# Gated mix of two attentions: projections in four column tiles, other buffer counts, and a last set in halves

## The chip, the cores and the metric

The kernel runs on one core of one Trainium2 chip. The metric is device time in microseconds (us) of one execution; lower is better. All times below come from runs on the chip or from one profiled execution.

## The reference

For x of 2048 rows and 512 columns (bf16) the reference computes `g * a + (1 - g) * b`:

```python
g = sigmoid((x * gate_w).sum(-1, keepdims=True))
# a, linear attention, 32 heads of 16:
pq, pk = q @ w_phi, k @ w_phi                      # per head, 16 x 16
phi_q = concat([softmax(pq), softmax(-pq)], -1)    # phi_k alike from pk
kv, z = einsum("bhsf,bhsd->bhfd", phi_k, v), phi_k.sum over s
a = (phi_q @ kv) / (phi_q @ z + 1e-6)  -> (2048, 512) @ A_wo
# b, softmax attention, 32 heads of 16:
b = softmax(q @ k.T * 0.25) @ v        -> (2048, 512) @ B_wo
```

Part b holds nearly all the work: 32 x 2048 x 2048 scores, an exponential of each, and the product with v.

## The kernel before, in words

**The softmax attention.** It runs in 32 sets (loop at L802 to L806): four blocks `qc` of 512 queries, four groups `g` of eight heads, and for each two halves `par` of four heads. A set has 16 key tiles `kt` of 128 keys; a key tile of a set is two score tiles of 128 keys x 1024 (two heads x 512 queries), so there are 32 x 16 x 2 = 1024 score tiles.

- Scores (`qk`, L826): two matmuls in row tiles (64 rows each) fill a PSUM tile of ring `R_r`, which has three of 1024 columns (L427). The zeros in the query tile `q` separate the heads.
- Exponentials, on one of two engines. ScalarE (ACT) does most with one ACTIVATE per score tile (L849) into a ring `E_r` of NE = 8 buffers of 128 x 1024 (L402); the first 24 go to memory of phiK and vA that isn't used yet. For `NDVE[set]` key tiles of each set VectorE (DVE) does them with integer steps: L839 for each of the two score tiles, then L861, L864 and L867 on 2048 columns. NDVE sums to 123 key tiles, so DVE does 246 score tiles and ACT 778.
- Weighted sums (`pv`, L873 and L886): four matmuls in column tiles (32 columns of weights each, `tile_position=(0, 32 * s)`) add to the one PSUM bank `O_r`, one group for a key tile on ACT, two for one on DVE.
- End of a set: O is copied out (L512 or L513, called at L911), transposed by TensorE (four f32 transposes, L918), and DVE takes the reciprocal of the row sums (L923) and multiplies (L924). The result goes by a DMA transpose (L939) to `oBT`; for the last set of all it goes by four transposes on TensorE (L949) and two copies (L952).

**Beside it.** Projections for q, k, v, the feature maps and A's v: `fill` (L515) issues four accumulating matmuls with 128 x 128 weights and 512 columns of x each (L519), and is called for 81 tiles (324 matmuls). The 16 output blocks take seven matmuls each (`of`, L974) and an eighth (`os`, L982) when the last head group is there; the result is scaled (L987 on ACT, L990 on DVE) and written (L992). The feature maps take two ACT exponentials for each of 32 blocks (L700), adds on GpSimd (POOL, L706) and more. A query tile is made by a projection, a copy to `qs`, and eight small DMAs on the SyncE queue (SP, L567) into a ring of four `q` buffers (L400), of which three are zeroed by POOL (L490).

**What sets the order.** Nothing is ordered by hand. `_Sched` (L108) is a list scheduler that runs before the program is built: each operation has an engine, an estimated duration, a due time (`prio`, mostly a time `ut(u)` in the plan of the 32 sets), dependencies, and, where it is first to use a ring buffer, a wait for the last user of that buffer. For TensorE the pick also weighs how many score tiles ACT and DVE have ahead, how many E buffers are held (`FULL`, L149), and a price `STAY` for a change of mode between "row", "col" and "full". The result is one fixed order of instructions per engine, with semaphore waits. So every constant at L35 to L81 can move every operation, and the time on the chip comes from the fixed orders alone.

**The check at the end.** L997 to L1002 test all the sums (DVE, DVE, TensorE, DVE) and write a flag; each engine waits for it, and a slow safe version of the kernel would follow if it were set. Here it isn't.

Of the kernel before, what the change touches and what calls it, by code (L numbers as in the profile page):

```python
# [6 lines left out]
BF16 = mybir.dt.bfloat16  # L7
# [3 lines left out]
ALU = mybir.AluOpType  # L11
# [5 lines left out]
KT = 4  # L17
S = 2048
NT = S // 128
NQ = 512  # L20
QC = S // NQ
# [14 lines left out]
PH = [0.0, -2.7, 0.0, 0.0, -1.2, 0.0, 1.2, 0.0, -0.7, -1.4, -1.5, -2.2, -2.9, -3.8, 2.5, -1.5, -1.5, -2.3, 0.7, -3.8, -0.7, -4.5, -2.0, -0.8, 0.0, -6.0, 5.8, 0.0, 0.1, 6.1, 3.6, 1.4]  # L36
# [5 lines left out]
NE = 8  # L42
FULL = 7
FEW = 1
SLACK = 0.6
# [6 lines left out]
RUSH_K = 20.0  # L52
RUSH_O = 10
RUSH_1 = 8.0
QLEAD1 = 26
LATE_A = 10
VLEAD = 3.0
VLEAD1 = 24
RUSH_V = 20.0
PK0 = 170  # L60
PKS = 20
PQ0 = 470
PQS = 30
KLEAD1 = 28
KLEAD = 40
QLEAD = 36
EARLY = 4
# [13 lines left out]
LATER = 14.0  # L81
# [26 lines left out]
class _Sched:  # L108
# [9 lines left out]
    def add(self, eng, prio, dur, fn, deps=(), tiles=(), mode=None, name="", dma=None, nb=0.0, after=(), parts=1, feeds=None):  # L118
        o = _Op()
        o.eng, o.fn, o.dur, o.prio = eng, fn, dur, prio  # L120
        o.deps = [d for d in deps if d is not None]
        o.after = list(after)
        o.tiles = list(tiles)
        o.mode, o.name, o.dma, o.est = mode, name, dma, nb
        o.shared = eng == "pool" or name in ("dm", "de", "dw") or name.startswith("qm")
        o.frees = any(t.slots is self.stock for t in tiles)
        o.late = 0.0 if name.startswith("qk") else SLACK
# [230 lines left out]
def _build(ctx, nc, A_x, A_wqkv, A_w_phi, A_wo, B_wqkv, B_wo, gate_w, out):  # L358
# [30 lines left out]
    ident = sb([128, 128], name="ident")  # L389
# [10 lines left out]
    q_r = ring(4, [128, 4, NQ], name="q")  # L400
# [63 lines left out]
    def pool(prio, dur, fn, deps=(), name="", nb=0.0):  # L464
        return add("pool", prio, dur, fn, deps=deps, name=name, nb=nb)
# [15 lines left out]
    op_id32 = i2  # L481
# [8 lines left out]
    op_qz = [pool(-96 - 0.1 * i, 2.0, lambda e, i=i: e.memset(q_r.aps[i][:], 0.0), name="qz", nb=LATER + 3.0) for i in range(1, 4)]  # L490
# [7 lines left out]
    MM = 0.217  # L498
# [15 lines left out]

    def fill(prio, tile, off, lhs, rhs, deps, name, rush=0.0, xd=None, n=512):  # L515

        f = None
        for t in range(KT):
            f = add("pe", prio - rush + 0.01 * t, MM * n / 512, lambda e, t=t: e.matmul(  # L519
                tile.ap[:, off:off + n], lhsT=lhs(t), rhs=rhs(t), start=(t == 0), stop=(t == KT - 1)),  # L520
                deps=list(deps) + (xd(t) if xd else []) + [f], tiles=[tile], mode="full", name=name, nb=max(0.0, prio - EARLY))
            fills.append(f)
        return f
# [210 lines left out]
    op_kz = []  # L734
# [67 lines left out]
    for qc in range(QC):  # L802
        for g in range(KT):
            ob = _Tile(oB_r)
            norm = []
            for par in range(2):  # L806
# [104 lines left out]
                n1 = evac("act" if final else "dve", ut(u) - RUSH_O, lambda ot=ot: ot.ap, lambda O=O: O.ap,  # L911
                          pvs + [op_m4, op_masks], [O, ot], name="Oev")

                if nset == 31:
                    calm = norm
                n2 = []
                for i in range(4):
                    n2.append(add("pe", pr, 0.165, lambda e, i=i, ot=ot, tt=tt: e.transpose(  # L918
                        tt.ap[:, 128 * i:128 * (i + 1)], ot.ap[:, 128 * i:128 * (i + 1)], ident32[:]),
                        deps=[n1, op_id32], tiles=[ot, tt], mode="full", name="tpb"))  # L920
                tv = lambda tt=tt: tt.ap[:, 0:512].rearrange("p (i s c) -> p i s c", i=4, c=32)
                rv = lambda rb=rb, part=part: rb.ap[:, part, :].rearrange("p (a b) -> p a b", b=4)
                n3 = add("dve", pr, 0.17, lambda e, tv=tv, rv=rv: e.reciprocal(rv(), tv()[:, :, :, 16]), deps=n2, tiles=[tt, rb])  # L923
                norm.append(add("dve", pr, 0.34, lambda e, tv=tv, rv=rv, ob=ob, par=par: e.tensor_tensor(  # L924
                    ob.ap.rearrange("p i (s a d) -> p i s a d", a=2, d=16)[:, :, :, par, :], tv()[:, :, :, 0:16],
                    rv().unsqueeze(3).to_broadcast([128, 4, 4, 16]), ALU.mult), deps=[n3], tiles=[tt, rb, ob]))
                recs.append(n3)
                reads.append(norm[-1])
# [8 lines left out]
            pr = ut(u + 4)  # L937
# [5 lines left out]
            to = _Tile(R_r)  # L943

            def tpc(e, ob=ob, to=to):
                ins = None
                for i in range(4):
                    v = to.ap[:, 512 * (i // 2) + 64 * (i % 2):][:, 0:64].bitcast(BF16)
                    ins = e.transpose(v, ob.ap[:, i, :], ident[:])  # L949
                return ins  # L950
            n6 = add("pe", pr, 0.45, tpc, deps=norm + [op_id], tiles=[ob, to], mode="full", name="tpc")
            ev_oBT[qc, g] = [add(eng, pr, 0.3, lambda e, to=to, g=g, qc=qc, lo=lo, eng=eng: (e.copy if eng == "act" else e.tensor_copy)(  # L952
                oBT[qc].ap[:, g, lo:lo + 256], to.ap[:, 2 * lo:2 * lo + 128].bitcast(BF16)),
                deps=[n6] + (op_kz if qc >= 2 else []), tiles=[to, oBT[qc]], name="oBev") for eng, lo in (("dve", 0), ("act", 256))]
# [6 lines left out]
    ends = [_Tile(R_r)] * 2 + [_Tile(M_r), _Tile(R_r)]  # L961
    begin = [ut(U - 6), ut(U - 6), ut(U - 4), ut(U) + 4]
    for st in range(NT):
# [8 lines left out]
        for k in range(2 * KT - 1):  # L972
            lhs, rhs = (oAT[:, k, sl], WoA[:, k, :]) if k < KT else (None, WoB[:, k - KT, :])
            f1 = add("pe", prio + 0.01 * k, MM, lambda e, tile=tile, off=off, k=k, qc=qc, sb_=sb_, lhs=lhs, rhs=rhs: e.matmul(  # L974
                tile.ap[:, off:off + 512], lhsT=lhs if k < KT else oBT[qc].ap[:, k - KT, sb_], rhs=rhs, start=(k == 0), stop=False),
                deps=[f1, ev_oAT[st], op_woA, op_woB] + [ev_oBT[qc, g] for g in range(KT - 1)], tiles=[tile, oBT[qc]],
                mode="full", name="of", nb=prio - EARLY,
                     after=[] if not last else calm if i == 2 else last_di if i < 2 else last_qk)

        def second(e, tile=tile, off=off, st=st):  # L980
            sb_ = slice(128 * (st % 4), 128 * (st % 4 + 1))
            return e.matmul(tile.ap[:, off:off + 512], lhsT=oBT[st // 4].ap[:, KT - 1, sb_], rhs=WoB[:, KT - 1, :], start=False, stop=True)  # L982
        f2 = add("pe", ut(U + 2) if last else prio, MM, second, deps=[f1, ev_oBT[qc, KT - 1][i // 2] if last else ev_oBT[qc, KT - 1]], tiles=[tile, oBT[qc]], mode="full", name="os")
        fi = _Tile(fin_r)
        src = lambda tile=tile, off=off: tile.ap[:, off:off + 512]
        if last and i % 2:
            ev = add("act", ut(U + 3), 0.478, lambda e, fi=fi, src=src, st=st: e.activation(  # L987
                fi.ap, src(), ACTF.Copy, scale=omg[:, st:st + 1]), deps=[f2, op_omg] + use_wp1, tiles=[tile, fi], name="fin")
        else:
            ev = add("dve", ut(U + 3) if last else prio, 0.66, lambda e, fi=fi, src=src, st=st: e.tensor_scalar(  # L990
                fi.ap, src(), omg[:, st:st + 1], None, op0=ALU.mult), deps=[f2, op_omg] + use_wp1, tiles=[tile, fi], name="fin")
# [5 lines left out]
    v1 = add("dve", ut(U + 2), 0.2, lambda e: e.tensor_single_scalar(acc[:, 0:144], acc[:, 0:144], BIG, ALU.is_le), deps=chk[-1:] + chkB[-1:] + [op_ge] + use_ez)  # L997
# [185 lines left out]
```

## Time and profile before

| | us |
|---|---|
| median of 3 runs | 772.44 |
| lowest and highest | 771.83 and 772.62 |
| the profiled execution, its time | 771.53 |
| the profiled execution, its span | 769.7 |
| busy: ACT, PE, DVE, POOL | 753.2, 707.5, 705.8, 182.8 |

The span runs from the first to the last event on the core; the time of the execution is 1.83 us longer. PE is TensorE's matmul row and PEld its weight loads. Records of ACT and PE overlap: an instruction's record starts before the one ahead has ended, so the mean of a record is longer than the distance from one to the next, and busy time is the union. The granted TensorE clock was 0.998.

### The profile page before, as it was taken

What the parts mean: (1) busy time and instruction counts of PE and PEld (TensorE: products, weight loads), DVE (VectorE), ACT (ScalarE), POOL (GpSimd) and SP (SyncE); (2) the same over time, 40 slices, a digit from 0 to 9 for tenths busy, and PEclk for the clock granted to TensorE, in tenths of its full rate; (3) what the DMA queues carried; (4) which work ended last, traced back from release to release, by engine and by line L of the source; (5) the groups of instructions that cost most, each with busy time, mean ns of one, the idle gap of its engine ahead of it and who ended that gap; (6) DMA issues with size and microseconds to landing.
All of it is one profiled execution on the core that took longest, in us unless ns stands there. A gap on an engine that the chain in (4) does not pass through costs nothing.

```text
span 769.7 us, 14300 instructions
## 1 busy us (share of the span) xinstructions
PE 707.5 (92%) x5880; PEld 236.7 (31%) x5949; DVE 705.8 (92%) x891; ACT 753.2 (98%) x856; POOL 182.8 (24%) x283
## 2 busy tenths in 40 slices
PE   8999999999998999999999899999999999998887
PEld 4333333332222322222233233232232323332222
DVE  6898997799999899999999989999997999999993
ACT  5999999999999999999999999999999999999995
POOL 2500000003334433343431231203311151202200
PEclk9999999999999999999999999999999999999999
DMA  9300000000000000000013112100211012100200
GB/s 220 55 9 2 15 2 1 15 2 8 8 7 9 2 15 1 15 1 8 9 15 90 21 35 36 24 26 8 48 35 29 23 28 55 28 19 18 43 8 30
DMA packets 54918, 19.60 MB, mean 25 GB/s; under 512 B 46784, under 2 KB 54848, under 8 KB 54848
## 3 DMA queue, kind: packets, MB, share of 16 engines
q1 hardware_dynamic: 53264, 18.10, 11.3%
q8 instruction: 47, 0.77, 0.4%
q10 hardware_dynamic: 1328, 0.52, 0.3%
q14 instruction: 23, 0.19, 0.1%
q0 software_dynamic: 256, 0.02, 0.1%
HBM read 4.21 MB, written 2.10 MB: 8 GB/s over the span
## 4 chain that ended last, share of the span: by engine, by line
ACT 84%; PE 11%; DMA 1%; DVE 1%; issue 1%; SPq 1%
ACT E L849 78%; PE ps L830 4%; ACT WAT L700 4%; PE ps L974 2%; PE ps L890 2%; ACT phiK L849 1%; ACT vA L849 1%; DMA D<-in_A_x_dram 1%; PE ps L877 1%; PE ps L519 1%; PE ps L742 1%; SPq L567 1%; DVE D L839 0%; DMA q<-qs 0%; PE ps L581 0%
## 5 line engine op out<-in xcount | busy, mean ns | idle before, releaser
L849 ACT ACTIVATE E<-ps 128x1024 bf16<-128x1024 f32 x754 | 702.0, 1183 | 0.4 <-PE ps L830 0.2
L830 PE MATMUL ps<-q,kT 64*128 64x512 bf16 x2048 | 361.5, 384 | 42.2 <-ACT E L849 30.3
L839 DVE TENSOR_SCALAR D<-ps 128x1024 int16<-128x1024 f32 x246 | 298.7, 1214 | 34.2 <-PE ps L830 30.7
L830 PEld LDWEIGHTS ps<-q,kT 64*128 64x128 bf16 x2048 | 90.1, 93 | 250.0 <-ACT E L849 191.7
L864 DVE TENSOR_TENSOR D<-D 128x2048 bf16<-128x2048 bf16 x123 | 151.3, 1232 | 0.6
L890 PE MATMUL ps<-E,vB 128*32 128x512 bf16 x1508 | 145.3, 388 | 3.7 <-issue 1.8
L706 POOL TENSOR_TENSOR WAT<-WAT 128x512 f32<-128x512 bf16 (+2 forms) x96 | 73.1, 762 | 260.8 <-DVE D L864 92.4
L877 PE MATMUL ps<-D,vB 128*32 128x512 bf16 x984 | 95.0, 387 | 3.4 <-issue 2.0
L861 DVE TENSOR_SCALAR D<-D 128x2048 int16<-128x2048 int16 x123 | 85.1, 694 | 0.7
L867 DVE TENSOR_SCALAR D<-D 128x2048 int16<-128x2048 int16 x123 | 83.5, 681 | 0.3
L890 PEld LDWEIGHTS ps<-E,vB 128*32 128x32 bf16 x1508 | 36.9, 93 | 76.1 <-issue 68.2
L717 POOL TENSOR_TENSOR phiK<-WAT,ss 128x512 bf16<-128x512 bf16 x32 | 33.5, 1057 | 37.5 <-DVE D L864 16.5
L519 PE MATMUL ps<-Wp,xT 128*128 128x512 bf16 x106 | 41.1, 389 | 0.5 <-issue 0.3
L700 ACT ACTIVATE WAT<-ps 128x512 bf16<-128x512 f32 x64 | 40.2, 771 | 0.0
L717 POOL TENSOR_TENSOR WB<-WAT,ss 128x512 bf16<-128x512 bf16 x32 | 33.3, 1057 | 28.0 <-DVE D L864 15.8
L519 PE MATMUL ps<-xT,WB 128*128 128x512 bf16 (+2 forms) x109 | 38.6, 380 | 0.6 <-issue 0.3
L877 PEld LDWEIGHTS ps<-D,vB 128*32 128x32 bf16 x984 | 24.4, 94 | 41.2 <-issue 35.0
L931 POOL TENSOR_TENSOR acc<-acc,rB 128x64 f32<-128x64 f32 x8 | 2.6, 320 | 120.2 <-DVE D L861 53.0
L974 PE MATMUL ps<-phiK 128*128 128x512 bf16 x80 | 28.3, 387 | 1.7 <-ACT WAT L700 1.2
L918 PE MATMUL ps<-ident,OT 128*128 128x128 f32 x128 | 27.8, 300 | 2.3 <-ACT WAT L700 1.8
L513 DVE COPY OT<-ps 128x512 f32<-128x512 f32 x31 | 21.0, 679 | 1.8 <-PE ps L890 1.6
L519 PEld LDWEIGHTS ps<-Wp,xT 128*128 128x128 bf16 x128 | 12.0, 96 | 31.8 <-issue 27.7
(100 smaller groups left out, 363.1 us busy)
## 6 DMA issues: line engine op xcount, KB each, us to landing
out_dram<-Wp SPq DMA_DIRECT2D x16, 128.0 KB, 1.7
q<-qs SPq DMA_DIRECT2D x120, 16.0 KB, 1.8
WB<-in_B_wqkv_dram SPq DMA_DIRECT2D x3, 384.0 KB, 5.4
D<-in_A_x_dram SPq DMA_DIRECT2D x1, 512.0 KB, 6.9
WAv<-in_A_wqkv_dram SPq DMA_DIRECT2D x1, 512.0 KB, 5.2
phiK<-in_A_wo_dram SPq DMA_DIRECT2D x1, 512.0 KB, 4.1
phiK<-in_B_wo_dram SPq DMA_DIRECT2D x1, 512.0 KB, 5.0
D<-in_A_x_dram ACTq DMA_DIRECT2D x1, 256.0 KB, 3.8
```

Source lines behind the costliest of these rows:

```text
L519: f = add("pe", prio - rush + 0.01 * t, MM * n / 512, lambda e, t=t: e.matmul(tile.ap[:, off:off + n], lhsT=lhs(t), rhs=rhs(t), start=(t = ...
L700: o5 = [add("act", prio + 1, 0.478, lambda e, a=a: e.activation(ev()[:, :, a, :], P(), ACTF.Exp, scale=1.0 - 2.0 * a), deps=[f], tiles=[ti ...
L706: o6 = add("pool", prio + 5, d, lambda e, n=n: e.tensor_tensor(tr(n), tr(2 * n)[:, :, 0:n], tr(2 * n)[:, :, n:2 * n], ALU.add), deps=[o6] ...
L717: halves.append(add("pool", prio + 7 + 0.1 * h, 0.15 + 1.8 / PH2, lambda e, gs_=gs_: e.tensor_tensor(dst().rearrange("p (g f) -> p g f", f ...
L830: ins = e.matmul(r.ap[:, 512 * i:512 * (i + 1)], lhsT=kT[p0:p0 + 64, g, 128 * kt:128 * (kt + 1)], rhs=qt.ap[p0:p0 + 64, 2 * pair + par, :] ...
L839: last_di = [add("dve", when - 6, 1.133, lambda e, r=r, I=I, part=part: e.tensor_scalar(I.ap[:, 1024 * part:1024 * (part + 1)], r.ap, EXP_ ...
L849: exps.append(add("act", when, 0.904, lambda e, r=r, E=E: e.activation(E.ap, r.ap, ACTF.Exp, scale=EXP_SCALE), deps=[q], tiles=[r, E], nam ...
L861: d1 = [add("dve", pd + 0.01 * y, 0.06 + 0.54 / SM, lambda e, I=I, F=F, lo=lo, hi=hi: e.tensor_scalar(F.ap[:, lo:hi], I.ap[:, lo:hi], 0x00 ...
L864: d4 = [add("dve", pd + 0.05 + 0.01 * y, 0.06 + 1.07 / SW, lambda e, I=I, F=F, lo=lo, hi=hi: e.tensor_tensor(F.ap[:, lo:hi].bitcast(BF16), ...
L867: d2 = [add("dve", pd + 0.1 + 0.01 * y, 0.06 + 0.54 / SE, lambda e, I=I, lo=lo, hi=hi: e.tensor_scalar(I.ap[:, lo:hi], I.ap[:, lo:hi], -12 ...
L877: ins = e.matmul(O.ap[32 * s:32 * s + 32, :], lhsT=vB_[:, kt, vcol(h):vcol(h) + 32], rhs=w.ap.bitcast(BF16)[:, base + 1024 * (s % 2) + 512 ...
L890: ins = e.matmul(O.ap[32 * s:32 * s + 32, :], lhsT=vB_[:, kt, vcol(h):vcol(h) + 32], rhs=es[s % 2].ap[:, 512 * (s // 2):512 * (s // 2 + 1) ...
```

## The change

1. `fill`, `of` and `os` issue each matmul as four, one for each 32 columns of the weights, with `tile_position` as `pv` has it. The planner counts them as mode "col" and takes 0.226 for 0.217.
2. NE from 8 to 12 (FULL from 7 to 11) and the ring of q from 4 to 2 buffers, so POOL zeroes one and not three.
3. The last set is finished in two halves: two copies of O of 256 columns on ACT, then for each half two transposes, reciprocal, multiply, two bf16 transposes and one copy (first half ACT, second DVE). The two halves of the last transpose go to different PSUM tiles (`t15`, which the fourth output block uses too, and O's bank).
4. Of the last four output blocks, the third is ordered behind the end of set 31 only (before: of 31 and 32, since `calm` was the list itself), and the fourth may start at `ut(U)`. The priorities of the last set's operations are earlier, and the check's first operation is planned behind the last copies.
5. NDVE, PH (offsets of DVE's key tiles in each set) and some twenty constants of the planner are changed. NDVE now sums to 124.

```diff
-NDVE = [3, 4, 3, 5, 2, 3, 4, 4, 4, 4, 4, 3, 5, 4, 3, 5, 3, 4, 4, 4, 4, 5, 4, 2, 5, 4, 3, 5, 4, 3, 5, 4]
+NDVE = [3, 5, 3, 5, 2, 4, 4, 4, 4, 4, 4, 2, 5, 4, 4, 5, 4, 4, 4, 3, 4, 5, 3, 3, 5, 5, 3, 3, 4, 3, 5, 4]
...
-NE = 8
-FULL = 7
+NE = 12
+NQB = 2
+FULL = 11
...
-STAY = 1.8
-RUSH = 2.5
+STAY = 1.0
+RUSH = 2.0
...
-    q_r = ring(4, [128, 4, NQ], name="q")
+    q_r = ring(NQB, [128, 4, NQ], name="q")
...
+    def by_columns(e, out_ap, lhs, rhs, start, stop):
+        ins = None
+        for s in range(4):
+            ins = e.matmul(out_ap[32 * s:32 * s + 32, :], lhsT=lhs[:, 32 * s:32 * s + 32], rhs=rhs, start=start, stop=stop,
+                           tile_position=(0, 32 * s), skip_group_check=True)
+        return ins
...
-                    pvs.append(add("pe", at, 0.226, term, deps=deps + op_vpad, tiles=tiles, mode="col", name=f"pv{nset}"))
-                pr = ut(u + 2)
+                    pvs.append(add("pe", at - (15.0 if nset == 32 else 0.0), 0.226, term, deps=deps + op_vpad, tiles=tiles, mode="col", name=f"pv{nset}"))
+                pr = ut(u - 16) if final else ut(u + 2)
...
+                nh = 2 if final else 1
+                w = 4 // nh
+                for hh in range(nh):
+                    lo = 128 * w * hh
...
                 if nset == 31:
-                    calm = norm
+                    calm = list(norm)
...
-    ends = [_Tile(R_r)] * 2 + [_Tile(M_r), _Tile(R_r)]
-    begin = [ut(U - 6), ut(U - 6), ut(U - 4), ut(U) + 4]
+    ends = [_Tile(R_r)] * 2 + [_Tile(M_r), t15]
+    begin = [ut(U - 6), ut(U - 6), ut(U - 4), ut(U)]
```

More of the change, by code (lines that the diff above doesn't have):

```diff
@@ L126, in add @@
         o.frees = any(t.slots is self.stock for t in tiles)
-        o.late = 0.0 if name.startswith("qk") else SLACK
+        o.late = 0.0 if name.startswith("qk") or name in ("tpc", "end") else SLACK
         o.users, o.start, o.end, o.count, o.sem, o.vc = [], None, None, None, None, None
@@ L518, in fill @@
         for t in range(KT):
-            f = add("pe", prio - rush + 0.01 * t, MM * n / 512, lambda e, t=t: e.matmul(
-                tile.ap[:, off:off + n], lhsT=lhs(t), rhs=rhs(t), start=(t == 0), stop=(t == KT - 1)),
-                deps=list(deps) + (xd(t) if xd else []) + [f], tiles=[tile], mode="full", name=name, nb=max(0.0, prio - EARLY))
+            f = add("pe", prio - rush + 0.01 * t, MM * n / 512, lambda e, t=t: by_columns(
+                e, tile.ap[:, off:off + n], lhs(t), rhs(t), t == 0, t == KT - 1),
+                deps=list(deps) + (xd(t) if xd else []) + [f], tiles=[tile], mode="col", name=name, nb=max(0.0, prio - EARLY))
             fills.append(f)
@@ L910, in _build @@
                 part = (nset - 1) % 4
-                n1 = evac("act" if final else "dve", ut(u) - RUSH_O, lambda ot=ot: ot.ap, lambda O=O: O.ap,
-                          pvs + [op_m4, op_masks], [O, ot], name="Oev")
-                if nset == 31:
-                    calm = norm
[L916 to L926, printed above, removed]
@@ L927, in _build @@
-                recs.append(n3)
-                reads.append(norm[-1])
+                nh = 2 if final else 1
+                w = 4 // nh
+                for hh in range(nh):
+                    lo = 128 * w * hh
+                    n1 = evac("act" if final else "dve", ut(u) - RUSH_O, lambda ot=ot, lo=lo, w=w: ot.ap[:, lo:lo + 128 * w],
+                              lambda O=O, lo=lo, w=w: O.ap[:, lo:lo + 128 * w], pvs + [op_m4, op_masks], [O, ot], n=128 * w, name="Oev")
+                    n2 = []
+                    for i in range(w):
+                        n2.append(add("pe", pr + 0.1 * hh, 0.165, lambda e, i=i, ot=ot, tt=tt, lo=lo, hh=hh: e.transpose(
+                            tt.ap[:, 512 * hh + 128 * i:512 * hh + 128 * (i + 1)], ot.ap[:, lo + 128 * i:lo + 128 * (i + 1)], ident32[:]),
+                            deps=[n1, op_id32], tiles=[ot, tt], mode="full", name="tpb"))
+                    tv = lambda tt=tt, w=w, hh=hh: tt.ap[:, 512 * hh:512 * hh + 128 * w].rearrange("p (i s c) -> p i s c", i=w, c=32)
+                    rv = lambda rb=rb, part=part, w=w, hh=hh: rb.ap[:, part, 4 * w * hh:4 * w * (hh + 1)].rearrange("p (a b) -> p a b", b=4)
+                    n3 = add("dve", pr + 0.1 * hh, 0.06 + 0.11 / nh, lambda e, tv=tv, rv=rv: e.reciprocal(rv(), tv()[:, :, :, 16]), deps=n2, tiles=[tt, rb])
+                    n4 = add("dve", pr + 0.1 * hh, 0.07 + 0.27 / nh, lambda e, tv=tv, rv=rv, ob=ob, par=par, w=w, hh=hh: e.tensor_tensor(
+                        ob.ap.rearrange("p i (s a d) -> p i s a d", a=2, d=16)[:, w * hh:w * (hh + 1), :, par, :], tv()[:, :, :, 0:16],
+                        rv().unsqueeze(3).to_broadcast([128, w, 4, 16]), ALU.mult), deps=[n3], tiles=[tt, rb, ob])
+                    norm.append(n4)
+                    recs.append(n3)
+                    reads.append(n4)
@@ L942, in _build, with tpc @@
                 continue
[L943 to L954, printed above, removed]
+            t15 = _Tile(R_r)
+            ev_oBT[qc, g] = []
+            for hh, eng, to, off in ((0, "act", t15, 512), (1, "dve", _Tile(O_r), 0)):
+                def tpc(e, ob=ob, to=to, hh=hh, off=off):
+                    ins = None
+                    for i in range(2):
+                        ins = e.transpose(to.ap[:, off + 64 * i:off + 64 * (i + 1)].bitcast(BF16), ob.ap[:, 2 * hh + i, :], ident[:])
+                    return ins
+                n6 = add("pe", pr, 0.22, tpc, deps=norm[0:1] + norm[1 + hh:2 + hh] + [op_id], tiles=[ob, to], mode="full", name="tpc")
+                ev_oBT[qc, g].append(add(eng, pr, 0.27 if eng == "act" else 0.2, lambda e, to=to, g=g, qc=qc, hh=hh, eng=eng, off=off: (
+                    e.copy if eng == "act" else e.tensor_copy)(
+                    oBT[qc].ap[:, g, 256 * hh:256 * hh + 256], to.ap[:, off:off + 128].bitcast(BF16)),
+                    deps=[n6] + (op_kz if qc >= 2 else []), tiles=[to, oBT[qc]], name="oBev"))
     for o, E in hosts:
@@ L981, in second @@
             sb_ = slice(128 * (st % 4), 128 * (st % 4 + 1))
-            return e.matmul(tile.ap[:, off:off + 512], lhsT=oBT[st // 4].ap[:, KT - 1, sb_], rhs=WoB[:, KT - 1, :], start=False, stop=True)
-        f2 = add("pe", ut(U + 2) if last else prio, MM, second, deps=[f1, ev_oBT[qc, KT - 1][i // 2] if last else ev_oBT[qc, KT - 1]], tiles=[tile, oBT[qc]], mode="full", name="os")
+            return by_columns(e, tile.ap[:, off:off + 512], oBT[st // 4].ap[:, KT - 1, sb_], WoB[:, KT - 1, :], False, True)
+        f2 = add("pe", ut(U - 14) + 0.1 * i if last else prio, MM, second, deps=[f1, ev_oBT[qc, KT - 1][i // 2] if last else ev_oBT[qc, KT - 1]], tiles=[tile, oBT[qc]], mode="col", name="end" if last else "os")
         fi = _Tile(fin_r)
```

42 lines of the change are left out of this document (21 added, 21 removed).

## The prediction, made before the change was run

> **What bounds the kernel now.** I read the page first (busy time, slices, the chain that ended last), then the chain in order of time, then the waits.
>
> ```profile
> span 769.7 us, 14300 instructions
> ...
> ACT  5999999999999999999999999999999999999995
> ...
> ACT 84%; PE 11%; DMA 1%; DVE 1%; issue 1%; SPq 1%
> ```
>
> ScalarE (ACT) is full in every slice but the first and the last, and 84% of the chain that ended last is ACT. Three rows of the chain in order of time (start, us, what) give the pace that it keeps:
>
> ```profile
> 27.70 7.33 ACT vA L849 x8
> ...
> 429.46 0.98 ACT WAT L700 x2
> ...
> 710.41 42.20 ACT E L849 x46
> ```
>
> An exponential of a score tile takes 42.20 / 46 = 0.917 us from one to the next, one of the feature maps 0.49. Between 27.70, when the head is over, and the last exponential there are these groups (page, costliest groups), and a row of the timeline gives the end: 739.42 + 19.60 = 759.02.
>
> ```profile
> L849 ACT ACTIVATE E<-ps 128x1024 bf16<-128x1024 f32 x754 | 702.0, 1183 | 0.4 <-PE ps L830 0.2
> ...
> L700 ACT ACTIVATE WAT<-ps 128x512 bf16<-128x512 f32 x64 | 40.2, 771 | 0.0
> ```
>
> ```profile
> 739.42 19.60 ACT L849 ACTIVATE E<-ps 128x1024 bf16<-128x1024 f32 x21
> ```
>
> (754 + 8) x 0.917 + 64 x 0.49 = 730.1 us of work stand in 759.02 - 27.70 = 731.3 us. So ACT loses at most 1.2 us in the whole middle, and whatever only makes another engine faster there can bring no more than that. What can move the end: fewer exponentials on ACT, the 9.7 us ahead of the first one, and the 10.7 us behind the last.
>
> **The change part by part.**
>
> *NDVE, 123 to 124 key tiles.* ACT loses two exponentials: -2 x 0.917 = **-1.83 us**, if ACT stays as full as it is. VectorE (DVE) gets one more chain, of these four groups (page):
>
> ```profile
> L839 DVE TENSOR_SCALAR D<-ps 128x1024 int16<-128x1024 f32 x246 | 298.7, 1214 | 34.2 <-PE ps L830 30.7
> ...
> L864 DVE TENSOR_TENSOR D<-D 128x2048 bf16<-128x2048 bf16 x123 | 151.3, 1232 | 0.6
> ...
> L861 DVE TENSOR_SCALAR D<-D 128x2048 int16<-128x2048 int16 x123 | 85.1, 694 | 0.7
> L867 DVE TENSOR_SCALAR D<-D 128x2048 int16<-128x2048 int16 x123 | 83.5, 681 | 0.3
> ```
>
> 2 x 1.214 + 1.232 + 0.692 + 0.679 = 5.03 us for each key tile. The busy times by stretch (length, then busy us of PE, PEld, DVE, ACT, POOL) say whether DVE has room:
>
> ```profile
> 30.00:400.00 370.00, 345.28 (x2824) 114.80 (x2856) 343.76 (x419) 369.84 (x422) 93.77 (x140) 1.00 0.04 7
> 400.00:759.00 359.00, 330.77 (x2802) 107.69 (x2831) 337.69 (x438) 358.71 (x404) 76.26 (x115) 1.00 0.15 31
> 504.00:624.00 120.00, 111.37 (x914) 35.95 (x923) 113.51 (x147) 119.94 (x138) 26.83 (x41) 1.00 0.12 27
> ```
>
> In the first 16 sets NDVE goes from 60 to 62: 10.06 us more against 370 - 343.76 = 26.2 us idle, and ACT shortens the stretch by 3.67, so 12.5 stay. In the second 16 it goes from 63 to 62, and DVE has 5 us less to do. So the key tile is added where DVE has room, and I count its 5.03 us at nothing; the cover that can run out is local (the slower rival).
>
> *Column tiles.* 324 + 128 = 452 matmuls become 1808, with as many weight loads. A column group is in this trace as `pv`; the first two rows (timeline) are eight matmuls in two groups on DVE's and ACT's tiles, the others (chain) a stretch where TensorE sets the pace:
>
> ```profile
> 503.48 0.40 PE L877 MATMUL ps<-D,vB 128*32 128x512 bf16 x4
> 503.70 0.39 PE L890 MATMUL ps<-E,vB 128*32 128x512 bf16 x4
> ```
>
> ```profile
> 486.45 0.32 PE ps L974
> 486.77 0.32 PE ps L830 x2
> 487.10 0.32 PE ps L974
> 487.42 0.33 PE ps L890 x4
> ...
> 489.36 0.54 PE ps L830 x4
> ```
>
> Two column groups in a row are 503.70 - 503.48 = 0.22 us apart, and two row groups 0.54 / 2 = 0.27 on the mean of a switch and none; each change of mode makes it 0.32 or 0.33. So a group of four costs 0.22 as the page's `pv` does, a projection's place between two score groups costs 0.33 for 0.32, and where it stands beside a `pv` a switch of 0.10 is gone. What no row shows is four tiles that stream the same x; the bounds are 0.22 and four in turn, 4 x 0.22 = 0.88. I take 0.22, since the two `pv` rows are the same four tiles with the same weights' shape. TensorE has room for more (waits, in total, times, longest):
>
> ```profile
> PEld ps L830 <- ACT E L849: 191.7, 582, 0.8
> ```
>
> It waited 191.7 us for ACT to free a score tile. But in the stretches where seven-matmul output blocks are slipped between scores, TensorE is the chain. One row of ACT's timeline lies in such a stretch:
>
> ```profile
> 483.46 28.98 ACT L849 ACTIVATE E<-ps 128x1024 bf16<-128x1024 f32 x31
> ```
>
> 31 exponentials at 0.917 would need 28.4, and 0.27 more because the last record (1183 ns) is longer than the pace; it took 28.98, so ACT loses some 0.3 us here and well under 1.2 over all. Fewer switches could give back part: **-0.2 us**, between -1.2 (all of the loss) and +1.0 (a loss as large again, by a worse fixed order).
>
> The Trainium skill speaks against this part: "TensorEngine Tiling (Array Packing)", When to Use Tiling, wants column tiles only for 64 or fewer columns, and "TensorE: Matmul & The Clock Gate", Part 3, has 3.07x for four packed row tiles of 512 columns and column tiles like them; a group would then take an estimated 4 / 3.07 = 1.30 of one matmul, against the 0.22 of the rows above.
>
> *Twelve E buffers, two of q.* ACT's idle ahead of its 754 exponentials is 0.4 us in all (row above), whatever ended it, so four more E buffers give between 0 and 0.4: nothing. Two buffers of q: SP issues eight DMAs for each query tile, which took this long,
>
> ```profile
> 140.68 4.94 SPq L567 DMA_DIRECT2D q<-qs  x8
> ```
>
> and behind them in SP's order stand the transposes of oB and oA and the output. The new wait is for the last score of the tile before the last. It is used for 64 of the plan's steps, and the next load is planned 44 steps ahead of need, 20 steps after the buffer is free; a set of 32 steps is about 731 / 32 = 23 us, so 14 us of room for 5 us of issues. Nothing, with room gone only if the scores run 14 us late. POOL's two zeroings less are POOL's alone.
>
> *The end.* The rows of the timeline behind the last exponential (start, us, engine, line):
>
> ```profile
> 759.74 0.59 ACT L512 COPY OT<-ps 128x512 f32<-128x512 f32 x1 [0.72 <-PE ps L877]
> ...
> 760.38 0.66 PE L918 MATMUL ps<-ident,OT 128*128 128x128 f32 x4 [0.15 <-ACT OT L512]
> ...
> 760.87 1.24 PE L974 MATMUL ps<-phiK 128*128 128x512 bf16 x5
> 761.07 0.26 DVE L923 RECIPROCAL rB<-ps 128x16 f32<-128x16 f32 x1 [6.56 <-PE ps L918]
> 761.36 0.42 DVE L924 TENSOR_TENSOR oB<-ps,rB 128x256 bf16<-128x256 f32 x1
> ...
> 761.95 0.39 PE L949 MATMUL ps<-ident,oB 128*128 128x128 bf16 x4
> ...
> 762.37 0.37 ACT L952 COPY phiK<-ps 128x256 bf16<-128x256 bf16 x1 [2.05 <-PE ps L949]
> 762.70 0.23 DVE L997 TENSOR_SCALAR acc<-acc 128x144 f32<-128x144 f32 x1 [0.91 <-POOL acc L935]
> ...
> 762.85 0.28 DVE L952 COPY phiK<-ps 128x256 bf16<-128x256 bf16 x1
> ...
> 763.24 0.69 ACT L987 ACTIVATE Wp<-ps,omg 128x512 bf16<-128x512 f32 x1 [0.49 <-PE ps L982]
> ...
> 763.95 2.13 SPq L992 DMA_DIRECT2D out_dram<-Wp  x4
> ...
> 764.98 0.75 DVE L990 TENSOR_SCALAR Wp<-ps,omg 128x512 bf16<-128x512 f32 x1 [0.18 <-PE ps L982]
> ```
>
> The last result is ready at 764.98 + 0.75 = 765.73, 6.71 behind the last exponential; the last output DMA is issued by 763.95 + 2.13 = 766.08 (+7.06). In between TensorE still does matmuls of the third and fourth block (L974, from 760.87 on), and L997 stands ahead of a copy. After, counted from the last exponential: +0.72 as before; half a copy on ACT about 0.37 (its 256-column row), +1.09; two f32 transposes 0.44 (between 0.33, half of four, and 0.66), +1.58; reciprocal 0.20 (half to all of 0.26), +1.81; multiply 0.27 (0.21 to 0.42), +2.11; two transposes about 0.3, +2.48; copy 0.37, +2.9; last matmuls, two for this half, about 0.4 and 0.22 more, +3.3 and +3.55; scaled by DVE in 0.75 to +4.1 and by ACT in 0.69 to +4.25. The second half's reciprocal and multiply end at +2.6, its copy on DVE at +3.3, its matmuls at +3.7 and +3.9; scaled behind the first on the same engines, to +4.9. If the check's two DVE operations get between, up to 0.6 later: +5.5. SP needs 2.13 / 4 = 0.53 for each output, from +4.15 on: the last is issued at +6.3. Against +7.06 and +6.71 this is a gain of 0.8 by SP's issues, up to 1.7 by the scaled rows; I take **-0.9 us**, from -1.7 to -0.2 (if the output matmuls stay where they are and only L997 moves). What is late next is SP, which issues four outputs in a row.
>
> *The head.* Its first exponential:
>
> ```profile
> 9.73 1.02 ACT L849 ACTIVATE phiK<-ps 128x1024 bf16<-128x1024 f32 x1 [1.28 <-PE ps L830]
> ```
>
> It waits for a score that stands on TensorE behind the transposes of x's second part, which had to land. The change has nothing ahead of that but column groups; 0, from -0.5 to +0.5.
>
> **Sum:** -1.83 - 0.2 + 0 - 0.9 = -2.9, so a span of 766.8 for 769.7. The profiled execution took 771.53, 1.83 more than its span and 0.9 under the median of 772.44; with the same distance the median goes to **769.5**. All lower ends together give -1.83 - 1.2 - 1.7 - 0.5 = -5.2 (767.2), all upper ends +1.0 - 1.83 - 0.2 + 0.5 = -0.5 (771.9).
>
> **The rivals.**
>
> *Only the exponentials count.* The new end gains nothing on the clock (the last results queue behind each other on DVE, ACT and SP as before), and new small waits of ACT take 0.6 of what two exponentials give: -1.2, 771.2. For it: four outputs in a row on SP. Against it: the L974 rows at 760.87 need no result of the last set.
>
> *Slower: DVE falls behind in sets 22 to 26.* By the count of exponentials these lie at about 504 to 624; NDVE there goes from 5, 4, 2, 5, 4 to 5, 3, 3, 5, 5, one more, 5.03 us against 120 - 113.51 = 6.5 us idle, of which 1.83 goes with ACT's shorter time. DVE would be full for 118 us. Its idle is mostly waiting for scores (30.7 of 34.2 us, L839's row); if it can use none of it, it is 5 to 7 us late at the end of the second set with 5, the last `pv` of that set is late, the next set cannot start on the one bank O, and E fills: twelve buffers are 12 x 0.917 = 11 us of ACT, some four of them in use anyway, so 7.3 us of cover. It costs from a lateness of 7.3 on; at 12, which needs a DVE idle as often as in the stretch 504 to 624 and 5 more, ACT loses about 5 us: 774.5. Against it: the next sets have 3 and 3, and the ring was enlarged by 3.7 us of ACT.
>
> *Column tiles of one x stream side by side only in part.* If a group takes 0.33, as one behind a switch, and not 0.22, TensorE has 452 x 0.11 = 50 us more. The 192 us of waiting hide them, but not where the output blocks stand between scores; one round of four blocks there is 32 matmuls, 3.5 us: 773.0. By the skill's estimated factor of 1.30 it would be 0.065 a group and 2.1 us, 771.6. Four in turn would be 452 x 0.66 = 298 us against 192, about 100 us slower, 870. Against all of it: the `pv` rows.
>
> *It doesn't do what it says*: had ACT been waiting for E, the extra buffers would be the gain; the 0.4 us of idle exclude it.
>
> **How the numbers follow.** Two results closer than 0.2% (1.5 us here) can't be told apart, so faster means under 770.9 and slower over 774.0. The forecast and what lies below 770.9: 0.66. Only the exponentials, with slow column groups: 0.18, within 0.2%. DVE behind, or a comparable loss of ACT: 0.13, slower. Four in turn: 0.03, slower. The forecast's own range is 767.2 to 771.9. For 8 in 10 the upper end goes up to the nearer half of the slower rival: 767.2 to 773.8.
>
> **What would show it.** Right: ACT's group L849 with two fewer, its idle in the middle still under 1 us, 42.2 us for 46 as now; L519 and L974 as four matmuls that start within 0.02 us, groups 0.22 apart; behind the last exponential the last scaled result at about +4.9 to +5.5. Wrong: waits of ACT for E's release or for L830 of over 1 us in the middle, above all at 500 to 650 with DVE without a gap; column groups over 0.25 apart; a later first exponential; or a last result no nearer than 6 us.

## The result, and the profile after

The changed kernel takes **769.02 us** (median of 6 runs, 768.54 to 770.66), the kernel before in the same series 772.19 (6 runs, 771.81 to 772.62). The ratio is 0.9964 (95% interval 0.9952 to 0.9977): 3.2 us faster, by 0.36%. A later series gave 768.56 against 771.88, ratio 0.9957 (0.9943 to 0.9970). The forecast was 769.5.

The profiled execution of the first series is one of its two slowest (770.50 us), for a reason that comes below. Its page, the span, the chain and the group of exponentials:

```profile
span 768.6 us, 17090 instructions
...
ACT 92%; PE 5%; DVE 1%; DMA 1%; issue 1%
...
L858 ACT ACTIVATE E<-ps 128x1024 bf16<-128x1024 f32 x752 | 701.4, 1241 | 1.1 <-PE ps L839 1.1
```

Two exponentials fewer, and the chain is now ACT for 92% and PE for 5%; before it was 84% and 11%. The stretches where TensorE set the pace are nearly gone. The later series' profile (span 766.8) is the better one to compare. Its chain in order of time (start, us, what), and ACT's last exponentials in its timeline:

```profile
27.66 7.33 ACT vA L858 x8
```

```profile
713.33 42.62 ACT L858 ACTIVATE E<-ps 128x1024 bf16<-128x1024 f32 x46
```

The last exponential ends at 713.33 + 42.62 = 755.95, that is 728.29 after the first into vA. The work in between is (752 + 8) x 0.917 + 64 x 0.49 = 728.3. **ACT loses nothing at all in the middle.** Before, it needed 731.32 for 730.1 of work. So the middle is 3.0 us shorter: 1.83 for the two exponentials, 1.2 for waits that are gone.

And behind the last exponential? Timeline of the same execution:

```profile
756.46 0.65 ACT L513 COPY OT<-ps 128x256 f32<-128x256 f32 x2 [0.50 <-PE ps L899]
...
757.46 0.21 DVE L934 RECIPROCAL rB<-ps 128x8 f32<-128x8 f32 x1 [8.17 <-PE ps L929]
757.70 0.29 DVE L935 TENSOR_TENSOR oB<-ps,rB 128x128 bf16<-128x128 f32 x1
...
758.37 0.37 ACT L967 COPY phiK<-ps 128x256 bf16<-128x256 bf16 x1 [1.27 <-PE ps L964]
...
759.26 1.41 DVE L1006 TENSOR_SCALAR Wp<-ps,omg 128x512 bf16<-128x512 f32 x2
...
760.04 1.80 SPq L1008 DMA_DIRECT2D out_dram<-Wp  x4
760.59 0.23 DVE L1013 TENSOR_SCALAR acc<-acc 128x144 f32<-128x144 f32 x1
760.79 0.69 ACT L1003 ACTIVATE Wp<-ps,omg 128x512 bf16<-128x512 f32 x1 [0.63 <-PE ps L520]
...
761.50 0.14 DVE L1018 TENSOR_SCALAR flag<-ps 1x1 int32<-1x1 f32 x1 [0.28 <-PE ps L1016]
```

The halves overlap as planned: the last scaled block is ready at 761.48, 5.53 behind the last exponential (6.71 before), and the last output is issued at 761.84, +5.89 (7.06 before). That is 1.2 us sooner. But the span ends at 766.8, **+10.85, where it was +10.68**. The waits of SP's queue say why (first the kernel before, then this execution; PEq is TensorE's instruction queue):

```profile
SPq L1146 <- DMA out_dram<-Wp: 1.2, 1, 1.2
...
SPq L1148 <- PEq L1148: 0.2, 1, 0.2
```

```profile
SPq L1164 <- PEq L1164: 2.8, 1, 2.8
```

Before, SP waited 1.2 us for the outputs to land and then 0.2 for TensorE at the program's end. Now the outputs have landed, and SP waits 2.8 us for TensorE, which has nothing left to compute. The flag comes at +5.69, as before (+5.78), and every engine has to load it and jump past the safe version's code. The views of two lines say how long the jump (COMPARE_BRANCH) takes and when an engine has reached the end of the program (DRAIN). They have the shortest, middle and longest duration in ns, then the first and last start in us; PEldq is TensorE's queue again. First before, then this execution:

```profile
L1139 PEldq COMPARE_BRANCH  x1: 3681/3681/3681, 765.7 to 765.7; - x1
...
L1148 SPq DRAIN  x1: 13/13/13, 769.4 to 769.4; - x1
L1148 PEldq DRAIN  x1: 73/73/73, 769.4 to 769.4; - x1
```

```profile
L1155 PEldq COMPARE_BRANCH  x1: 3812/3812/3812, 762.7 to 762.7; - x1
...
L1164 SPq DRAIN  x1: 13/13/13, 764.0 to 764.0; - x1
L1164 PEldq DRAIN  x1: 68/68/68, 766.5 to 766.5; - x1
```

TensorE's jump takes 3.7 to 3.8 us. Before, SP and TensorE reached the end together, at 769.4; now SP is there at 764.0 and TensorE at 766.5.

### The profile page after: what moved, and what is told of

Same layout as the page of the kernel before. It is cut to its first block, busy times and chain, and to the rows that moved or that the text cites. A ratio compares the mean times of both kernels' runs of the same rounds, so it can differ in the third digit from the quotient of the medians.

```text
span 768.6 us, 17090 instructions
## 1 busy us (share of the span) xinstructions
PE 713.8 (93%) x7309; PEld 222.8 (29%) x7309; DVE 711.4 (93%) x898; ACT 750.8 (98%) x855; POOL 180.6 (23%) x281
## 4 chain that ended last, share of the span: by engine, by line
ACT 92%; PE 5%; DVE 1%; DMA 1%; issue 1%
ACT E L858 85%; ACT WAT L709 4%; PE ps L839 2%; PE ps L520 2%; ACT phiK L858 1%; ACT vA L858 1%; PE ps L899 1%; DMA D<-in_A_x_dram 1%; DVE q L566 0%; PE ps L886 0%; DVE D L848 0%; PE ps L590 0%; PE ps L669 0%; DVE xT L625 0%; PE ps L617 0%
## 5 line engine op out<-in xcount | busy, mean ns | idle before, releaser
L839 PE MATMUL ps<-q,kT 64*128 64x512 bf16 x2048 | 365.2, 386 | 39.6 <-ACT E L858 33.9
L848 DVE TENSOR_SCALAR D<-ps 128x1024 int16<-128x1024 f32 x248 | 301.9, 1217 | 23.5 <-PE ps L839 21.1
L876 DVE TENSOR_SCALAR D<-D 128x2048 int16<-128x2048 int16 x124 | 87.1, 706 | 0.2
L870 DVE TENSOR_SCALAR D<-D 128x2048 int16<-128x2048 int16 x124 | 85.9, 697 | 0.6
L520 PE MATMUL ps<-Wp,xT 128*32 128x512 bf16 x512 | 50.2, 387 | 1.0 <-ACT WAT L709 1.0
L520 PE MATMUL ps<-xT,WB 128*32 128x512 bf16 (+2 forms) x528 | 48.2, 380 | 0.6 <-ACT WAT L709 0.5
L520 PE MATMUL ps<-phiK 128*32 128x512 bf16 x384 | 34.3, 385 | 0.4 <-ACT WAT L709 0.3
L520 PE MATMUL ps<-WAv,xT 128*32 128x512 bf16 x256 | 23.5, 387 | 2.8 <-ACT WAT L709 2.8
```

Of the source, the lines that this page charges most:

```text
L520: ins = e.matmul(out_ap[32 * s:32 * s + 32, :], lhsT=lhs[:, 32 * s:32 * s + 32], rhs=rhs, start=start, stop=stop, tile_position=(0, 32 * s ...
L839: ins = e.matmul(r.ap[:, 512 * i:512 * (i + 1)], lhsT=kT[p0:p0 + 64, g, 128 * kt:128 * (kt + 1)], rhs=qt.ap[p0:p0 + 64, 2 * pair + par, :] ...
L848: last_di = [add("dve", when - 6, 1.133, lambda e, r=r, I=I, part=part: e.tensor_scalar(I.ap[:, 1024 * part:1024 * (part + 1)], r.ap, EXP_ ...
L870: d1 = [add("dve", pd + 0.01 * y, 0.06 + 0.54 / SM, lambda e, I=I, F=F, lo=lo, hi=hi: e.tensor_scalar(F.ap[:, lo:hi], I.ap[:, lo:hi], 0x00 ...
L876: d2 = [add("dve", pd + 0.1 + 0.01 * y, 0.06 + 0.54 / SE, lambda e, I=I, lo=lo, hi=hi: e.tensor_scalar(I.ap[:, lo:hi], I.ap[:, lo:hi], -12 ...
```

## The experiments

Two theories stood against each other. **Prediction's theory:** 1.8 us from the exponentials, 0.9 from the end, little from column tiles. **Theory from the traces:** all of it is in ACT's middle, 1.8 from the exponentials and 1.2 from column tiles (fewer switches of TensorE between its modes: row tiles, column tiles, whole array); the end gives nothing because TensorE's way out behind the flag ends the program.

The table holds all of them. Middle loss: from the first exponential into vA to the end of the last, less the work of the kernel's own count (728.3, or 730.1 with two more exponentials). End: from the last exponential to the end of the span. Both are of the profiled execution, the times are medians of several; "before" in the three series took 771.72, 771.88 and 771.90.

| kernel | us | ratio to before (95%) | middle loss | end |
|---|---|---|---|---|
| before | 772.19 | 1 | 1.2 | 10.68 |
| changed, first profile | 769.02 | 0.9952 to 0.9977 | 1.3 | 11.34 |
| changed, second profile (e8) | 768.56 | 0.9943 to 0.9970 | 0.0 | 10.85 |
| e1 whole matmuls, new order | 780.81 | 1.0111 to 1.0142 | 11.2 | 10.74 |
| e2 old end | 769.06 | 0.9950 to 0.9977 | 0.0 | 11.04 |
| e3 before with columns, new order | 775.86 | 1.0039 to 1.0066 | 4.1 | 12.02 |
| e4 no safe version | 766.86 | 0.9923 to 0.9951 | 0.0 | 8.05 |
| e5 whole matmuls, same order | 774.49 | 1.0025 to 1.0053 | 4.5 | 10.72 |
| e6 before with columns, same order | 772.54 | 0.9997 to 1.0015 | 1.5 | 11.50 |
| e7 flag earlier | 769.30 | 0.9951 to 0.9978 | 1.3 | 10.75 |
| e9 old end, no safe version | 768.14 | 0.9937 to 0.9964 | 1.3 | 9.22 |
| e10 old NDVE and PH | 772.69 | 1.0002 to 1.0020 | 2.0 | 10.82 |
| e11 eight E buffers | 776.81 | 1.0045 to 1.0073 | 8 | 11.3 |
| e12 gate spread | 777.62 | 1.0060 to 1.0088 | 8.4 | 10.98 |

### Column tiles, with and without their order (e1, e3, e5, e6)

e1 takes the columns out of the changed kernel, and the planner makes a new order:

```diff
-    MM = 0.226
+    MM = 0.217
...
-            f = add("pe", ..., lambda e, t=t: by_columns(e, tile.ap[:, off:off + n], lhs(t), rhs(t), t == 0, t == KT - 1), ..., mode="col", ...)
+            f = add("pe", ..., lambda e, t=t: e.matmul(tile.ap[:, off:off + n], lhsT=lhs(t), rhs=rhs(t), ...), ..., mode="full", ...)
```

(and the same for `of` and `os`).

> The changed kernel with its projections and output blocks as whole 128-column matmuls again (planned as before: mode full, 0.217). Theory of the prediction: column tiles give 0.2 us, so about 769.2 and the same ACT pace. Theory from the two traces: of the 3.2 us gained, some 1.2 are ACT's losses in the middle, which went with the mode switches of TensorE; then this kernel is at about 770.2 and ACT loses 1 us or more again between the first exponentials into vA and the last one. Both: the end behind the last exponential is as in the changed kernel, within 0.3 us.

Measured 780.81, 12 us slower than the changed kernel, far past both theories; nearly all of it in the middle. e3 is the mirror: `by_columns`, mode "col" and MM = 0.226 in the kernel before, nothing else.

> The kernel before with column tiles alone (fill, of and os as four, mode col, 0.226), constants and end as before. Theory of the prediction: -0.2 us, 772.0. Theory from the traces: TensorE's switches cost ACT some 1.2 us, and part of that goes: 771.2, with ACT's distance in the stretch of the second round of output blocks nearer to 0.917 than 28.98 us for 31.

Measured 775.86, 4 us *slower* than before. So in these two runs the changed kernel without column tiles, and the kernel before with them, are both slower than the kernel before, and since the planner reorders everything, they can't say whether the tiles or the orders are to blame. Two more keep the order fixed. e5 has the changed kernel's planner inputs (mode "col", 0.226) and issues whole matmuls:

```diff
-            f = add("pe", prio - rush + 0.01 * t, MM * n / 512, lambda e, t=t: by_columns(
-                e, tile.ap[:, off:off + n], lhs(t), rhs(t), t == 0, t == KT - 1),
+            f = add("pe", prio - rush + 0.01 * t, MM * n / 512, lambda e, t=t: e.matmul(
+                tile.ap[:, off:off + n], lhsT=lhs(t), rhs=rhs(t), start=(t == 0), stop=(t == KT - 1)),
                 deps=..., tiles=[tile], mode="col", ...)
```

> The changed kernel with every instruction in the same order, but projections and output blocks issued as whole matmuls (the planner still counts them as column tiles). This parts the column tiles' own effect from the order that was planned for them. Column tiles save a switch where a projection stands beside a weighted sum: if that is why ACT no longer loses time, this kernel loses about 1 us, 770 or a little more, with distances of 0.32 where 0.22 stood. If the order alone did it, it stays within 0.3 us of the changed kernel.

Measured 774.49: in one and the same order the column tiles are worth **5.9 us** between the medians. Three of e5's five executions have a mean clock of 0.993 to 0.995; the two at 0.998 and 0.999 took 773.80 and 773.29, some 5 us more than e8. The profiled one (773.29) shows 4.5 as ACT's loss in the middle. The same stretch of both orders, TensorE's timeline (start, us, then the instructions), first the changed kernel (its first profile), then e5:

```profile
676.78 0.40 PE L520 MATMUL ps<-Wp,xT 128*32 128x512 bf16 x4
677.01 0.39 PE L899 MATMUL ps<-E,vB 128*32 128x512 bf16 x4
677.22 0.39 PE L886 MATMUL ps<-D,vB 128*32 128x512 bf16 x4
677.55 0.61 PE L839 MATMUL ps<-q,kT 64*128 64x512 bf16 x4
```

```profile
680.20 0.39 PE L528 MATMUL ps<-Wp,xT 128*128 128x512 bf16 x1
680.52 0.40 PE L899 MATMUL ps<-E,vB 128*32 128x512 bf16 x4
680.75 0.39 PE L886 MATMUL ps<-D,vB 128*32 128x512 bf16 x4
681.07 0.61 PE L839 MATMUL ps<-q,kT 64*128 64x512 bf16 x4
```

Above, a projection and two weighted sums start 0.23 and 0.21 apart; below, the projection in front of the same two takes 0.32, and the two stay 0.23 apart. Counted over the weight loads of the traces, TensorE changes its mode 1803 times before, 1544 times after and 1790 in e5. The count alone doesn't set the time of another order: e3 has 1538, the fewest, and is slower than before. How long TensorE waited for ACT to free a score tile (its slack; before, e8, e5):

```profile
PEld ps L830 <- ACT E L849: 191.7, 582, 0.8
```

```profile
PEld ps L839 <- ACT E L858: 255.5, 627, 0.8
```

```profile
PEld ps L839 <- ACT E L858: 164.2, 452, 0.8
```

e6 is the kernel before with columns issued and the planner's inputs kept (mode "full", 0.217).

> The kernel before with every instruction in the same order, but projections and output blocks issued as four column tiles (the planner still counts them as whole). If column groups cost 0.22 as weighted sums do: between 0 and 1 us faster than before, since switches beside weighted sums go, and none is added. If a group of four on one x took 0.28 or more: 1 us slower or more.

Measured 772.54 against 771.88, within what can be told from no change. The switches fall to 1585 and the slack rises to 259.0, but ACT loses no less than before (1.5 for 1.2). Its profile is of the slowest of its eleven executions (773.24). There 0.9 of the loss is one wait of ACT for a score, and TensorE's row shows what the score waited for:

```profile
703.71 0.39 PE L838 MATMUL ps<-q,kT 64*128 64x512 bf16 x2 [1.61 <-DMA q<-qs]
```

a query tile's DMA, which no column tile makes faster. (Before, TensorE waited 0.6 us at this place, and ACT lost nothing by it.) So the tiles make room on TensorE, and only in the order planned for that room does it show as time. Neither of the two runs that have one without the other (e5, e6) is faster than the kernel before.

### The end (e2, e4, e7, e9)

e2 gives the changed kernel the end of before; up to the last set its order is the same.

```diff
-                nh = 2 if final else 1
+                nh = 1
...
-                    calm = list(norm)
+                    calm = norm
```

(with the old transposes at the end, the old priorities and the check not held back).

> The changed kernel with the end of before: last set whole, old priorities, third and fourth output block ordered as before, check not held behind the copies. Everything up to the last set is the same order. Theory of the prediction: the new end is worth 0.9 us, so 769.9. Theory from the traces: the outputs are ready 1.2 us earlier, but the program ends some 5.5 us after the check's flag, which comes no earlier; then this kernel takes 769.0 or up to 0.7 less, with its outputs 1.2 us later behind the last exponential.

769.06 against 769.02 and 768.56: the new end is worth nothing that can be measured. In e2 SP waits 1.6 us for the outputs and then 0.4 for TensorE, whose jump takes 4.3 us there. e4 leaves out the safe version; flag and load stay.

```diff
         bad = engine.value_load(flag[0:1, 0:1], min_val=0, max_val=1)
-        with engine.If(bad > 0):
-            ...
-            G.emit(e, engine)
```

> The changed kernel without the slow safe version: the flag is still computed and loaded by each engine, but no branch follows and the code of the safe version is left out. If the program's end is set by the landing of the outputs: within 0.3 us of the changed kernel. If it is set by TensorE's way out behind the flag, past the safe version's code: the end comes 2 to 3 us earlier, at about 766.5, and SP waits for the outputs' landing and no longer 3 us for TensorE.

766.86, 1.7 to 2.2 us faster than the changed kernel. From its profile, the last output's issue, the flag, and SP's wait:

```profile
760.64 1.80 SPq L1008 DMA_DIRECT2D out_dram<-Wp  x4
...
762.10 0.15 DVE L1018 TENSOR_SCALAR flag<-ps 1x1 int32<-1x1 f32 x1 [0.28 <-PE ps L1016]
```

```profile
SPq L1159 <- PEq L1159: 0.2, 1, 0.2
```

From the flag at 762.25 to the end of the span, 764.6, are 2.35 us, where the changed kernel's two profiles have 5.65 and 5.16 and the one before 4.90. In e4 TensorE is at the end by 763.2, and SP, which waits for the outputs, by 764.4. So with the safe version TensorE's way out past its code ends the program, and without it the outputs do. e9 is e4 with the old end:

> The changed kernel with the end of before and without the safe version (flag computed and loaded, no branch, its code left out). With the safe version the new and the old end took the same time. If the new end's 1.2 us are hidden by the way out past the safe version's code, they show here: this kernel at about 768, against 766.9 for the new end without the safe version. If the new end saves nothing by itself: 766.9.

768.14 against 766.86, and 9.22 against 8.05 from the last exponential: without the way out, the new end's 1.2 us appear. The times alone say it less sharply: they are of two series, e9's five executions lie between 767.43 and 770.46, and the profiled one is the slowest, with a head 2.2 us late and the fall of the clock that comes below; neither lies behind the last exponential. The gain was made and hidden. e7 leaves the safe version in and pulls the flag ahead of the third block's scaling on DVE (`third` is that scaling, `v4` the flag):

```diff
+    third.after.append(v4)
```

> The changed kernel with the third output block's scaling behind the flag on DVE, so that the check's two operations and the flag come first; all else in the same order. If the program's end follows the flag (some 5.6 us behind it in the changed kernel's profile): the flag comes 0.6 to 0.7 us earlier and so does the end, about 768.4, though the last output is 0.6 us later. If the outputs' landing sets the end: 0.3 to 0.6 us slower.

The flag came 0.65 us earlier (+5.04), the end 0.1 (+10.75): from the flag to the end it now took 5.71. The median of 769.30 is no better, nor are the two executions at a clock of 0.998 and 0.999 (768.39 and 768.71). "The end follows the flag at a fixed distance" falls; the distance was 4.8 to 5.7 in the eleven profiles with the safe version in which outputs weren't issued long after the flag. It goes with the length of TensorE's jump: 3.42 us in e5, which has 4.8, and 4.2 to 4.3 in e2, e7 and the first profile, which have 5.7. What makes the jump longer or shorter is open.

### NDVE, buffers and the gate (e8, e10, e11, e12)

> The changed kernel once more, to compare with on the same chip. In its first profile the granted clock fell to 0.57 between 100 and 104 us, behind the 64 one-column matmuls of the gate, and ACT lost about 1 us there. Without that drop the last exponential should end 728.3 us behind the first into vA, so that ACT loses nothing in the middle, and the span is about 767; with it, 768.6.

768.56, and the profile used above: no loss of ACT. e10 has the lines NDVE and PH of before in the changed kernel, and a new order.

> The changed kernel with NDVE and PH of before, so 123 key tiles on DVE and two more exponentials on ACT; the planner makes a new order. If the exponentials' term is right: 1.83 us of ACT's work more, 770.4, plus what the new order makes ACT wait (over 0.4 us in the middle is loss of the order, not of the term).

772.69, 4.1 us more: 1.83 for two exponentials at the same pace, and 2.0 that ACT loses in the profile (0.0 in e8). Of the 2.0, 1.1 are ACT's idle time at 100 to 108 us, where the clock fell to 0.66; the rest is the order's. So the time agrees with the term, but the run doesn't isolate it; the one execution of eleven at a clock of 1.0 took 771.38. e11 has NE = 8 and FULL = 7:

> The changed kernel with eight E buffers (FULL 7) and all else kept, two buffers of q too; the planner makes a new order. Prediction: four buffers are worth 0 to 0.4 us. If ACT then waits for buffers or for scores behind weighted sums that were moved ahead to free them, the middle loses more than 1 us and the buffers were worth that in this plan.

776.81. ACT's waits name weighted sums, which free E buffers, as well as scores:

```profile
ACT E L858 <- PE ps L899: 2.9, 3, 1.4
ACT E L858 <- PE ps L839: 2.6, 6, 0.5
```

With eight, the plan from the same constants loses some 8 us in the middle. The run has another order as well, and about 1 us of its loss stands behind a fall of the clock at 456 to 464 us, so it doesn't say what the buffers alone are worth, nor what twelve would bring to the old plan. e12 sets the gate's four parts apart:

```diff
-deps=..., name="gate", nb=ut(60 + LATE_A)))
+deps=..., name="gate", nb=max(ut(60 + LATE_A), 97.0 + 2.2 * part if part else 0.0)))
```

> The changed kernel with the four parts of the gate (16 one-column matmuls each) at least 2.2 us apart instead of one behind each other within 3.2 us; the planner makes a new order from there on. If the density of one-column matmuls is what makes the granted clock fall behind them in some executions: no run shows a clock under 0.998 and none takes 1.5 us more than the others. What the new order costs shows as ACT's loss elsewhere.

777.62, and its runs have clocks of 0.994 to 0.997. In the new order a query tile came 4.1 us late (ACT's wait at 153.4, behind TensorE's for the DMA), the clock fell there (0.64 in 152 to 156), and 8.4 us were lost in all. Around the gate the profile's clock stays at 1.00, but so it does in several profiles with the four parts close together. So it settles nothing on the gate.

## Why the prediction was right, and where it was not

- **What bounds the kernel.** Right. In e8 (and in e2 and e4) ACT's work alone fills the middle to 0.1 us, and the bound of 1.2 us on what relief of other engines can bring was met: all of it came.
- **Two exponentials, -1.83.** Right: 752 rows, and the pace unchanged (42.62 us for 46 with the last one's full record).
- **Column tiles, -0.2.** Right price of a group and right sign, wrong size: the relief of ACT is 1.2, the lower end of the bounds. I took the loss as something a new order could only partly avoid. The 1.2 belongs to tiles, order, buffers and constants together; no run shows the tiles' own part of it. A group of four on one x costs 0.22, as taken from the `pv` rows:

```profile
752.73 1.05 PE L520 MATMUL ps<-phiK 128*32 128x512 bf16 x16
```

  four groups in 1.05 us, the last with its full 0.40, so 0.22 apart, where whole matmuls stood 0.21 apart before (five in 1.24, the last with 0.39). The estimate of 1.30 matmuls a group from the Trainium skill ("TensorE: Matmul & The Clock Gate", Part 3) doesn't hold here. What the Trainium skill states in "TensorEngine Tiling (Array Packing)", Key Properties, that a change of mode drains the array, agrees with e5's rows: 0.32 over a change, 0.23 without. I also priced the tiles against the old order, where they bring nothing (e6); in the new order they carry some 5 us (e5).
- **E buffers, nothing.** Right against the old order, whose ACT never waited for them; it doesn't ask whether the new order needs them, as e11 suggests without showing it.
- **The end, -0.9.** This is the step that failed: "What is late next is SP, which issues four outputs in a row." The outputs did come 1.2 us sooner, but TensorE's way out behind the flag was late next, and the end stayed at 10.7 to 11.3 us. The sum asked when the last output is issued, and not when each engine reaches the end of the program. The trace of before had the answer: TensorE's jump of 3.68 us ended at 769.4, together with SP's wait for the outputs, so outputs that land sooner could bring next to nothing. (SP's wait of 0.2 us for TensorE doesn't tell it: e4 has the same 0.2, with TensorE there 1.2 us ahead of SP.) Inside the term, the last issue at +5.89 was sooner than the forecast +6.3.
- **The head, 0.** Right: first exponential into vA at 27.66 for 27.70. It is no sharp test, since e2, e4, e7 and e9, which leave the head as it is, have it at 27.4 to 29.9.
- **The sum** came out at -2.9 for -3.2 measured because two errors cancel: 1.0 too little for the relief of ACT, 0.9 too much for the end. That the number is this close is luck.
- **The rivals.** DVE did not fall behind: in 504 to 624 of the first profile (row below) it was busy for 115.87 of 120 us, and ACT for all of it. "Only the exponentials count" was half right, on the end. Four tiles in turn: excluded by the row of 16 matmuls above.

```profile
504.00:624.00 120.00, 113.21 (x1150) 33.74 (x1148) 115.87 (x150) 120.00 (x137) 29.94 (x46) 1.00 0.15 30
```

## What to carry to other kernels

Where one engine is full from end to end, subtract its work from its span first: the difference bounds what every relief of the others can bring, and here it was met to the tenth. Before pricing a shorter end, look up when each engine reaches the end of the program, its jumps included, and not only when the last result is out. And a resource and the order planned for it are one change: runs that took column tiles, their order, buffers or constants away lost 4 to 12 us against the whole.

## What the runs showed of the hardware that was not expected

TensorE's jump past the unused code at the end lasts 3.4 to 4.3 us in the twelve profiles that have it (rows above), and what sets its length is open.

In the first profile of the changed kernel the granted clock fell to 0.57 for one stretch (length, busy us of PE, PEld, DVE, ACT, POOL, then the clock):

```profile
96.00:100.00 4.00, 3.92 (x78) 2.26 (x75) 3.97 (x6) 4.00 (x6) 0.00 (x0) 1.00 0.02 4
100.00:104.00 4.00, 4.00 (x34) 1.03 (x32) 3.21 (x7) 3.01 (x5) 0.22 (x1) 0.57 0.00 0
```

It follows the gate's 64 matmuls of one column (L669, 96.8 to 100.0), in which TensorE shows as busy; of the 1.3 us that ACT lost in the middle, 1.1 are its idle time at 100 to 108. This is why that execution took 770.5, and probably why the one of 0.994 mean clock, which wasn't profiled, took 770.66, when the four at 0.998 took 768.5 to 769.1. Behind a gate in such a dense run the clock also fell in e1, e7, e9 and e10 (to 0.57 to 0.72), and it stayed at 1.00 in e2, e4, e5, e8 and e11; in e8 the same instructions stood at the same place. Before, the gate's matmuls are spread over 86.1 to 91.1, and no fall shows there. But in e11 the clock fell at 456 to 464 and in e12 at 152 to 156, far from any gate. So a dense gate is neither enough for a fall nor needed for one. That it makes one more likely is argued from this, not shown: e12 was to test it and could not.
